# One load for a unit's q and k, row-wise exponentials for its first half, more idle products, and a new order table

## The chip, the cores and the metric

The kernel runs on one core of one Trainium2 chip. Such a core has TensorE for matrix products (PE in the profile; PEld is its loading of weights), VectorE (DVE), ScalarE (ACT), GpSimd (POOL), and SyncE (SP), which here only issues transfers to the 16 DMA engines. The metric is device time in microseconds for one launch. The kernel before was timed three times: 768.71, 768.9 and 770.37 us, median 768.9 us.

## The reference

Chunked attention over q, k and v of 8 batches, 8 heads, 576 positions and 64 dimensions, in chunks of 64, then a two-layer product with a gate:

```python
scores = scale * np.matmul(q_c, k_c.transpose(0, 1, 2, 4, 3))     # per chunk of 64: 64 x 64
scores = scores - np.max(scores, axis=-1, keepdims=True)
attn = np.exp(scores)
attn = attn / (np.sum(attn, axis=-1, keepdims=True) + 1e-09)
out = np.matmul(attn, v_c)
# x: the attention's output as 4608 tokens by 512; w_in 512 x 2048, w_out 2048 x 512
h = x @ w_in
g = h * np.clip(h + 3.0, 0.0, 6.0) / 6.0
return g @ w_out
```

## The kernel before

The 4608 tokens are nine blocks of 512. Each block has two attention units, named by block and half: 00, 01, 10, up to 81. A unit is 128 partitions (two heads of 64) by 8 chunks. Its chain is: load q and k, 64x64 products for the scores, row maximum, exponential, row sum, reciprocal, share (multiply by the reciprocal), turn (transpose), product with v, and keep (copy out of PSUM as x). All the large products are done in float32 as a high and a low part of each operand, with three passes of 128x512: high times high, high times low, low times high (`passes`, L544 to L546). The high part is a ScalarE copy and the low part a VectorE subtraction, so each operand needs one instruction on either engine before its second and third passes can start.

Block 0 is computed directly. Its first products (a0, then eleven more in single passes, L559) begin as soon as unit 00's x and the first weight are there. Blocks 1 to 8 go in four super-blocks (s = 0 to 3) of two blocks, each as a first product of seven quarter-size sums over w_in, gates, and a second product of seven sums over w_out. The operands of the second product are sums of gate tiles: t1 (L1217) and t2 (L1219) are differences and sums of two gate tiles in SBUF, done on GpSimd for s above 0 except where a list gives them to VectorE; m (L1257) are further sums on VectorE; each operand then gets its high copy on ScalarE (L1250, "uh") and its low subtraction on VectorE (L1254, "ul"). The gate itself is L1012, and L1196 adds two PSUM results; both read at least one operand from PSUM.

The order of every engine's instructions is written out: `DATES` holds one number per step, and `Schedule.order` sorts the steps by it. Steps are then issued in that order, each on its own engine, and semaphores hold an engine until the operands of its next instruction are ready. Engines take their instructions strictly in this order, so a step that waits holds all behind it on its engine.

Unit 00 and 01 are special (`class First`): the two heads of a unit are two halves a = 0 and a = 1 of 64 partitions, with own PSUM banks, so that the first half can run ahead. In the kernel before, unit 00's q and k come in two loads of 64 partitions (`load_rows`, L316: step qk00 and step qk00b), and its scores are two steps of 32 products each, one per half. Exponentials of both halves go the same way: a product with minus the identity subtracts the row maximum inside PSUM ("less", L502), one ScalarE instruction takes the exponential of 128x512 (L505), VectorE sums the rows (L508). The other way, by rows, exists for later units and, in `First`, for halves named in `BY_ROWS`, where no half stands yet: VectorE negates the maximum and ScalarE takes eight exponentials of 128x64 with the maximum as bias, each summing its row as it goes.

`warm_up(n)` issues products of a constant with itself that nobody reads: n counts bfloat16 products of 128x512, and four of them are replaced by one float32 product. `WARM` is the count at the program's start. `FILL` scales how many follow a TensorE step, by the planned gap behind it, until block 0's first product with v.

Of the kernel before, what the change touches and what calls it, by code (L numbers as in the profile page):

```python
# [9 lines left out]
F32 = mybir.dt.float32  # L10
# [32 lines left out]
WARM = 8  # L43
APIECE = ['00']
PIECE = 0.75
FILL = (2.0, 4.0)
# [16 lines left out]
LOADS = ['qk00', 'qk00b', 'qk01', 'wa0', 'v00', 'qk10', 'v01', 'wa1', 'wa2', 'wb0', 'v10', 'wa3', 'wb1', 'wa4', 'wb2', 'wb3', 'qk11', 'wa5', 'v11', 'wb4', 'wa6', 'wa7', 'wb5', 'wb6', 'wb7']  # L63
# [16 lines left out]
BY_ROWS = {'00': (), '01': ()}  # L80
# [95 lines left out]
"""  # L176


# [1230 lines left out]
```

## Time and profile before

| | us |
|---|---|
| median of three timed runs | 768.9 |
| the profiled execution, its own time | 769.79 |
| its span, first to last instruction | 768.0 |
| TensorE busy in it | 758.1 (99%) |
| VectorE, ScalarE, GpSimd busy | 586.4, 477.3, 70.6 |

The profile is one execution. Its time lies 0.89 us above the median of the timed runs, and 1.79 us of it lie outside the span. Busy shares are averages: what a stage costs is read from the timelines of that stage. A timeline row gives its start, its length, the engine, the source line, the operation with tile names (buffer numbers left out), shape, and how many equal instructions were merged. In brackets stands the idle time of the engine before it and what ended that. A float32 product shows as two MATMUL instructions, one pass of float32r or bfloat16 as one.

### The profile page before, as it was taken

The numbers are of one execution on the slowest core, as the hardware profiler recorded it, in microseconds if no ns is written. First come the engines' busy times: TensorE is split into PE (matmuls) and PEld (weight loads), VectorE is DVE, ScalarE is ACT, GpSimd is POOL, SyncE is SP. The second block draws the span as 40 slices with busy tenths as digits, with TensorE's granted clock in tenths as the row PEclk, the third lists the DMA queues.
The fourth block names the chain that finished last, engine by engine and source line by source line (L and its number), as shares of the span: only waits on it lengthen the run. The fifth ranks groups of instructions, "written<-read, shape, count | busy, mean of one in ns | idle before, by whom it ended". The sixth has DMA issues, their size and how long they took to land.

```text
span 768.0 us, 13863 instructions
## 1 busy us (share of the span) xinstructions
PE 758.1 (99%) x5443; PEld 621.8 (81%) x5443; DVE 586.4 (76%) x722; ACT 477.3 (62%) x918; POOL 70.6 (9%) x74
## 2 busy tenths in 40 slices
PE   8999999999999999999999999999999999999998
PEld 4788888888888888888888888888888888887787
DVE  3998999988999997636999785456898744368871
ACT  2998878597877756667853646667745444454430
POOL 0000000000000000012100110303000112044001
PEclk9999999999999999999999999999999999999999
DMA  9989999989998786976857586658566665565563
GB/s 316 420 332 351 352 323 339 326 279 294 326 338 306 245 331 204 330 260 207 287 197 258 207 310 224 243 195 276 174 222 217 217 226 191 200 200 182 185 213 117
DMA packets 68321, 200.14 MB, mean 261 GB/s; under 512 B 7136, under 2 KB 19680, under 8 KB 63904
## 3 DMA queue, kind: packets, MB, share of 16 engines
q1 hardware_dynamic: 65632, 191.00, 71.9%
q0 software_dynamic: 2480, 8.13, 2.8%
q8 instruction: 43, 0.70, 0.4%
q14 instruction: 22, 0.18, 0.1%
q10 hardware_dynamic: 144, 0.13, 0.1%
HBM read 154.14 MB, written 45.09 MB: 259 GB/s over the span
## 4 chain that ended last, share of the span: by engine, by line
PE 94%; DVE 4%; DMA 1%; ACT 1%; issue 1%; POOL 0%; DVEq 0%; ACTq 0%
PE acc L544 19%; PE acc L546 18%; PE acc L545 18%; PE h L544 11%; PE h L545 11%; PE h L546 11%; DVE wa L1254 2%; PE two L331 2%; PE h L435 2%; PE h L559 1%; DMA qk<-qk_in 1%; PE s L478 1%; DVE wb L1257 0%; PE two L435 0%; PE s L502 0%
## 5 line engine op out<-in xcount | busy, mean ns | idle before, releaser
L545 PE MATMUL acc<-wa,ws 128*128 128x512 f32 (+1 forms) x432 | 167.5, 388 | 1.2 <-DVE wa L1254 1.2
L544 PE MATMUL acc<-wa,ws 128*128 128x512 f32 (+1 forms) x432 | 168.3, 390 | 0.0
L546 PE MATMUL acc<-wa,ws 128*128 128x512 f32 (+1 forms) x432 | 167.5, 388 | 0.0
L1250 ACT CAST wa<-wb 128x1024 fp32r<-128x1024 f32 x96 | 97.5, 1052 | 59.7 <-DVE wb L1260 19.5
L1254 DVE TENSOR_TENSOR wa<-wb,wa 128x1024 fp32r<-128x1024 f32 x96 | 118.7, 1266 | 19.0 <-ACT wa L1250 19.0
L545 PE MATMUL h<-wa,ws 128*128 128x512 f32 (+1 forms) x248 | 95.8, 386 | 1.0 <-DVE wa L1254 1.0
L1011 ACT ACTIVATE wb<-acc,half 128x512 f32<-128x512 f32 x94 | 64.1, 692 | 52.5 <-DVE acc L1196 48.4
L544 PE MATMUL h<-wa,ws 128*128 128x512 f32 (+1 forms) x248 | 95.7, 386 | 0.0
L546 PE MATMUL h<-wa,ws 128*128 128x512 f32 (+1 forms) x248 | 95.7, 386 | 0.0
L545 PEld LDWEIGHTS acc<-wa,ws 128*128 128x128 f32 x432 | 81.2, 188 | 17.9 <-DVE wa L1254 1.6
L544 PEld LDWEIGHTS acc<-wa,ws 128*128 128x128 f32 x432 | 81.1, 188 | 17.1 <-DVE acc L1196 0.2
L546 PEld LDWEIGHTS acc<-wa,ws 128*128 128x128 f32 x432 | 81.1, 188 | 16.5
L1012 DVE SCALAR_TENSOR_TENSOR wb<-wb,acc 128x512 f32<-128x512 f32 x94 | 62.8, 680 | 24.3 <-ACT wb L1011 24.3
L1196 DVE TENSOR_TENSOR acc<-acc,p 128x512 f32<-128x512 f32 x47 | 32.6, 697 | 55.2 <-PE acc L546 39.6
L545 PEld LDWEIGHTS h<-wa,ws 128*128 128x128 f32 x248 | 46.6, 188 | 10.9 <-DVE wa L1254 1.5
L544 PEld LDWEIGHTS h<-wa,ws 128*128 128x128 f32 x248 | 46.6, 188 | 9.4
L546 PEld LDWEIGHTS h<-wa,ws 128*128 128x128 f32 x248 | 46.6, 188 | 9.3
L366 ACT ACTIVATE e<-two,m 128x64 f32<-128x64 f32 x160 | 48.6, 334 | 7.0 <-DVE m L360 4.9
L1012 DVE SCALAR_TENSOR_TENSOR wb<-wb,h 128x512 f32<-128x512 f32 x34 | 23.1, 683 | 27.6 <-ACT wb L1011 27.5
L1282 POOL DMA_DIRECT2D out_t<-o x17 | 9.4, 553 | 377.5 <-DVE g L1235 235.7
L1217 POOL TENSOR_TENSOR wb<-wb 128x512 f32<-128x512 f32 x18 | 26.0, 1453 | 192.4 <-DVE wb L1012 140.9
L366 ACT ACTIVATION_READ_ACCUMULATOR e<-two,m 128x1 f32 x160 | 36.4, 227 | 0.0
(276 smaller groups left out, 1429.0 us busy)
## 6 DMA issues: line engine op xcount, KB each, us to landing
ws<-b SPq DMA_DIRECT2D x84, 512.0 KB, 4.7
ws<-a SPq DMA_DIRECT2D x72, 512.0 KB, 4.8
qk<-qk_in SPq DMA_DIRECT2D x16, 1024.0 KB, 7.6
wa<-b SPq DMA_DIRECT2D x28, 512.0 KB, 6.9
a<-wa SPq DMA_DIRECT2D x44, 256.0 KB, 5.2
v<-v_in SPq DMA_DIRECT2D x17, 512.0 KB, 6.4
wa<-w_in_out SPq DMA_DIRECT2D x8, 1024.0 KB, 12.3
wb<-w_in_out SPq DMA_DIRECT2D x8, 1024.0 KB, 9.4
```

Of the source, the lines that this page charges most:

```text
L331: PE.matmul(self.s[to, a, 2 * i + k, :], lhsT=self.qk[rows, 0, 2 * i + s, o], rhs=self.qk[rows, 1, 2 * i + s, o], start=True, stop=True)
L366: ACT.activation(out=self.flat(self.e)[:, c], in_=self.flat(self.s)[:, c], func=AF.Exp, bias=self.m[:, c:c + 1], scale=SCALE, accum_out=se ...
L435: PE.matmul(po[s][o, a, i, :], lhsT=self.v[rows, a, i, o], rhs=self.aT[rows, a, i, o], start=not bank or a == i == 0, stop=True, skip_grou ...
L544: PE.matmul(ps, lhsT=a_h, rhs=b_h, start=first, stop=False, skip_group_check=more)
L545: PE.matmul(ps, lhsT=a_h, rhs=b_l, start=False, stop=False, skip_group_check=more)
L546: PE.matmul(ps, lhsT=a_l, rhs=b_h, start=False, stop=last, skip_group_check=more)
L1011: work.add("relu" + name, "ACT", 0.69, [after, *more], lambda: ACT.activation(out=out(), in_=ps(), func=AF.Relu, bias=half, scale=1.0 / 6. ...
L1012: work.add("gate" + name, "DVE", 0.69, ["relu" + name], lambda: DVE.scalar_tensor_tensor(out=out(), in0=out(), scalar=1.0, in1=ps(), op0=A ...
L1196: return lambda: DVE.tensor_tensor(out=t[to], in0=t[of], in1=t["p5"], op=ALU.add)
L1217: work.add(id_("t1."), *on[1:], [id_("gate3."), id_("gate2.")], lambda f=gq, on=on[0]: on.tensor_tensor(out=f(0, 1), in0=f(0, 1), in1=f(0, ...
L1250: ACT.copy(out=g_ops[s, i, pp][:, :, 0], in_=src())
L1254: work.add(low, *(("POOL", 2.5) if on else ("DVE", 1.22)), [high], lambda i=i, pp=pp, src=src, on=POOL if on else DVE: on.tensor_tensor(ou ...
```

## The change

Unit 00's q and k come in one load of 128 partitions; `load_rows`, the two-step scores of unit 00 and the constants for them go. Its first half takes its exponentials by rows. The program starts with 11 units of idle products in place of 8, rounded in another way, and `FILL` is 3.0 in place of 2.0 for gaps up to 3. All of `DATES` is replaced by a new table of 2298 numbers.

```diff
-WARM = 8
-APIECE = ['00']
-PIECE = 0.75
-FILL = (2.0, 4.0)
+WARM = 11
+FILL = (3.0, 4.0)
-LOADS = ['qk00', 'qk00b', 'qk01', 'wa0', ...
+LOADS = ['qk00', 'qk01', 'wa0', ...
-BY_ROWS = {'00': (), '01': ()}
+BY_ROWS = {'00': (0,), '01': ()}
 DATES = """
-0 95 226 357 619 881 1667 ...
+...
-            long = (n + 1) // 4
-            for x in [half] * long + [nought] * max(0, n - 4 * long):
+            long = n // 4
+            for x in [half] * long + [nought] * (n - 4 * long):
-        def load_rows(self, a, qk=None):
-            ...
-        def scores(self, part=(0, 1)):
-            if part[0] == 0:
-                self.s = [t.rearrange("p (c t) -> p c t", t=CH) for t in self.two(ps_b[self.dp])]
+        def scores(self):
+            self.s = [t.rearrange("p (c t) -> p c t", t=CH) for t in self.two(ps_b[self.dp])]
             for c in range(NB):
-                for a in part:
+                for a, rows in enumerate(HALF):
-            if u in APIECE:
-                work.add("scores0" + u, "PE", PIECE, ["qk" + u, *scores], lambda: a.scores((0,)), due=due)
-                work.add("scores" + u, "PE", PIECE, ["scores0" + u, f"qk{u}b"], lambda: a.scores((1,)), due=due)
-            else:
-                work.add("scores" + u, "PE", 1.30, ["qk" + u, *scores], a.scores, due=due)
+            work.add("scores" + u, "PE", 1.30, ["qk" + u, *scores], a.scores, due=due)
```

The first place is TensorE at the program's start, before. `h<-half` are idle products, `s<-qk` the scores of unit 00, `s<-xd` those of unit 01, `s<-m,minus` the subtraction of the maximum.

```order
L247 MATMUL h<-half 128x512 x2
L478 MATMUL s_175<-qk 64x64 x16
L247 LDWEIGHTS half
L247 MATMUL h<-half 128x512
L478 MATMUL s_176<-qk 64x64 x16
L502 MATMUL s_175<-m_162,minus 128x512
L502 MATMUL s_176<-m_163,minus 128x512
L478 MATMUL s_221<-xd 64x64 x2
```

The same place after the change (of the score rows, which alternate between the two halves' banks, the first pair of each unit).

```order
L245 MATMUL h<-half 128x512 x2
L245 LDWEIGHTS half
L245 MATMUL h<-half 128x512
...
L469 MATMUL s_177<-qk 64x64 x2
L469 MATMUL s_178<-qk 64x64 x2
...
L245 LDWEIGHTS half
L245 MATMUL h<-half 128x512
...
L469 MATMUL s_224<-xd 64x64 x2
L469 MATMUL s_225<-xd 64x64 x2
...
L493 MATMUL s_178<-m_166,minus 128x512
L493 MATMUL s_224<-m_169,minus 128x512
L493 MATMUL s_225<-m_170,minus 128x512
```

The first load's scores were two steps with one idle product between; now they are one step, with three idle products behind it, and unit 01's scores stand ahead of every subtraction of a maximum, of which unit 00's first half needs none.

The second place is VectorE at the start, before. `m<-s` is a row maximum, `z<-e` and `z<-xb` are the row sums of unit 00's two halves, the two rows on z that follow add 1e-9 and invert, `e<-e,z` is the share.

```order
L490 TENSOR_REDUCE m_162<-s_175 128x8
L235 TENSOR_SCALAR minus<-ident 128x128
L490 TENSOR_REDUCE m_163<-s_176 128x8
L508 TENSOR_REDUCE z_164<-e 128x8
L511 TENSOR_SCALAR z_164<-z_164 128x8
L512 RECIPROCAL z_164<-z_164 128x8
L515 TENSOR_TENSOR e<-e,z_164 128x512
L490 TENSOR_REDUCE m_166<-s_221 128x8
L490 TENSOR_REDUCE m_167<-s_222 128x8
```

After the change:

```order
L481 TENSOR_REDUCE m_165<-s_177 128x8
L233 TENSOR_SCALAR minus<-ident 128x128
L484 TENSOR_SCALAR m_165<-m_165 128x8
L481 TENSOR_REDUCE m_166<-s_178 128x8
L481 TENSOR_REDUCE m_169<-s_224 128x8
L481 TENSOR_REDUCE m_170<-s_225 128x8
L502 TENSOR_SCALAR z_167<-z_167 128x8
L503 RECIPROCAL z_167<-z_167 128x8
L499 TENSOR_REDUCE z_168<-xb 128x8
L506 TENSOR_TENSOR e<-e,z_167 128x512
```

The sum over `e` is gone, a negation of the maximum is new, and both maxima of unit 01 stand ahead of the first reciprocal.

The third place is the start of the second product of the last super-block (s = 3). First GpSimd, before: its last t1 (L1217, on the last pair of gate tiles) and the t2 (L1219) around it.

```order
L1217 TENSOR_TENSOR wb_1987<-wb_1987 128x512
L1219 TENSOR_TENSOR g_2656<-wb_3875,wb_3848 128x512
L1217 TENSOR_TENSOR wb_1451<-wb_1451 128x512
L1219 TENSOR_TENSOR g_2720<-wb_1658,wb_1451 128x512
L1219 TENSOR_TENSOR g_2656<-wb_3875,wb_3848 128x512
L1219 TENSOR_TENSOR g_2720<-wb_1658,wb_1451 128x512
L1219 TENSOR_TENSOR g_2644<-wb_2090,wb_1987 128x512
```

After the change (t1 is L1202, t2 is L1204):

```order
L1204 TENSOR_TENSOR g_2599<-wb_3874,wb_3860 128x512
L1202 TENSOR_TENSOR wb_1470<-wb_1470 128x512
L1204 TENSOR_TENSOR g_2599<-wb_3874,wb_3860 128x512
L1204 TENSOR_TENSOR g_2704<-wb_1546,wb_1470 128x512
L1202 TENSOR_TENSOR wb_1470<-wb_1470 128x512
L1204 TENSOR_TENSOR g_2681<-wb_2090,wb_2002 128x512
L1204 TENSOR_TENSOR g_2704<-wb_1546,wb_1470 128x512
```

Before, four t2 follow the last t1; now two do, and the other two stand ahead of it. VectorE at the same place, before, from the last gates of the first product on: L1254 is "ul", L1257 is "m".

```order
L1196 TENSOR_TENSOR acc<-acc,p_6755 128x512
L1012 SCALAR_TENSOR_TENSOR wb_1658<-wb_1658,acc 128x512
L1012 SCALAR_TENSOR_TENSOR wb_1451<-wb_1451,acc 128x512
L1254 TENSOR_TENSOR wa_6884<-wb_1987,wa_6884 128x2x512
L1254 TENSOR_TENSOR wa_6860<-g_2681,wa_6860 128x2x512
L1254 TENSOR_TENSOR wa_6872<-wb_1451,wa_6872 128x2x512
L1257 TENSOR_TENSOR wb_1451<-g_2720,wb_1451 128x2x512
L1257 TENSOR_TENSOR wb_3848<-g_2656,wb_3848 128x2x512
L1257 TENSOR_TENSOR wb_3604<-g_2681,wb_3604 128x2x512
L1257 TENSOR_TENSOR wb_1987<-g_2644,wb_1987 128x2x512
L1254 TENSOR_TENSOR wa_6915<-g_2720,wa_6915 128x2x512
L1254 TENSOR_TENSOR wa_6897<-g_2656,wa_6897 128x2x512
```

After the change (L1239 is "ul", L1242 is "m"):

```order
L1239 TENSOR_TENSOR wa_6846<-g_2506,wa_6846 128x2x512
L1181 TENSOR_TENSOR acc<-acc,p_6775 128x512
L997 SCALAR_TENSOR_TENSOR wb_1470<-wb_1470,acc 128x512
L1239 TENSOR_TENSOR wa_6889<-wb_1470,wa_6889 128x2x512
L1239 TENSOR_TENSOR wa_6833<-wb_2002,wa_6833 128x2x512
L1239 TENSOR_TENSOR wa_6901<-g_2599,wa_6901 128x2x512
L1239 TENSOR_TENSOR wa_6933<-g_2681,wa_6933 128x2x512
L1239 TENSOR_TENSOR wa_6924<-g_2704,wa_6924 128x2x512
L1242 TENSOR_TENSOR wb_3618<-g_2506,wb_3618 128x2x512
L1242 TENSOR_TENSOR wb_1470<-g_2704,wb_1470 128x2x512
L997 SCALAR_TENSOR_TENSOR wb_1546<-wb_1546,acc 128x512
L1242 TENSOR_TENSOR wb_3860<-g_2599,wb_3860 128x2x512
```

The four m stood ahead of all but one of the ul that read a t2 (`g`); now four of these stand ahead of every m. For s = 2 GpSimd makes ten such sums in either kernel: before, in the order t1, t1, t1, t2, t1, t1 and four t2, with the sixth on the last pair of gates; now t1, t2, t1, t2, t1, t1, t2, t1, t2, t2, with the second t1 on a pair of gates that VectorE makes late.

## Rows read from the trace of the kernel before

**Rows 1.** The page: busy time by engine, and its group of row-wise exponentials.
```profile
PE 758.1 (99%) x5443; PEld 621.8 (81%) x5443; DVE 586.4 (76%) x722; ACT 477.3 (62%) x918; POOL 70.6 (9%) x74
...
L366 ACT ACTIVATE e<-two,m 128x64 f32<-128x64 f32 x160 | 48.6, 334 | 7.0 <-DVE m L360 4.9
```

**Rows 2.** What TensorE waited for, 24 to 766 us: total, times, longest.
```profile
PE acc L545 <- DVE wa L1254: 1.2, 1, 1.2
PE h L545 <- DVE wa L1254: 1.0, 1, 1.0
```

**Rows 3.** Timeline of TensorE, start: start us, us, line, op, count, [idle before].
```profile
0.93 3.78 PE L247 MATMUL h<-half 128*128 128x512 f32 x4 [0.93 <-DVE half L232]
5.70 1.97 PE L478 MATMUL s<-qk 64*64 64x64 f32 x32 [0.99 <-DMA qk<-qk_in]
...
10.04 3.27 PE L502 MATMUL s<-m,minus 128*128 128x512 f32 x4
13.25 1.16 PE L478 MATMUL s<-xd 64*64 64x64 f32 x64
...
15.30 1.98 PE L502 MATMUL s<-m,minus 128*128 128x512 f32 x4
17.12 0.60 PE L247 MATMUL h<-half 128*128 128x512 bf16 x2
...
24.05 0.47 PE L559 MATMUL h<-xa,wa 128*128 128x512 f32 x1 [0.52 <-DVE wa L283]
```

**Rows 4.** DMA issues of the first 14 us: size, median us to landing.
```profile
qk<-qk_in SPq DMA_DIRECT2D x2, 512.0 KB, 5.8
xd<-qk_in SPq DMA_DIRECT2D x1, 1024.0 KB, 8.5
```

**Rows 5.** Two stretches by engine: us, busy, granted clock, DMA share, GB/s.
```profile
2.00:5.00 3.00, 2.71 (x4) 0.61 (x2) 0.00 (x0) 0.22 (x2) 0.00 (x0) 1.00 1.03 232
7.60:12.00 4.40, 4.40 (x38) 2.81 (x37) 1.52 (x3) 0.00 (x0) 0.00 (x0) 1.00 1.01 417
```

**Rows 6.** Timeline of VectorE, 12 to 24 us.
```profile
12.79 0.69 DVE L508 TENSOR_REDUCE z<-e 128x8 f32<-128x512 f32 x1 [1.93 <-ACT e L505]
...
13.95 0.69 DVE L515 TENSOR_TENSOR e<-e,z 128x512 f32<-128x512 f32 x1
14.56 1.28 DVE L490 TENSOR_REDUCE m<-s 128x8 f32<-128x512 f32 x2
...
17.09 0.69 DVE L508 TENSOR_REDUCE z<-g 128x8 f32<-128x512 f32 x1 [0.22 <-ACT g L505]
```

**Rows 7.** Timeline of ScalarE, 12 to 13 us.
```profile
12.16 0.60 ACT L505 ACTIVATE e<-s 128x512 f32<-128x512 f32 x1 [9.92 <-PE s L502]
```

**Rows 8.** Timeline of TensorE, 703 to 714 us.
```profile
705.94 0.50 PE L545 MATMUL acc<-wa,ws 128*128 128x512 f32 x1 [1.21 <-DVE wa L1254]
...
712.75 0.50 PE L545 MATMUL h<-wa,ws 128*128 128x512 f32 x1 [1.04 <-DVE wa L1254]
```

**Rows 9.** Timeline of GpSimd, 684 to 705 us.
```profile
684.20 1.30 POOL L1217 TENSOR_TENSOR wb<-wb 128x512 f32<-128x512 f32 x1 [8.16 <-DVE wb L1012]
...
697.79 7.00 POOL L1219 TENSOR_TENSOR g<-wb,wb 128x512 f32<-128x512 f32 x4
```

**Rows 10.** Timeline of VectorE, 676 to 716 us.
```profile
684.63 6.41 DVE L1254 TENSOR_TENSOR wa<-wb,wa 128x1024 fp32r<-128x1024 f32 x3
...
703.57 2.31 DVE L1254 TENSOR_TENSOR wa<-wb,wa 128x1024 fp32r<-128x1024 f32 x1
705.81 4.62 DVE L1257 TENSOR_TENSOR wb<-g,wb 128x1024 f32<-128x1024 f32 x4
710.35 3.48 DVE L1254 TENSOR_TENSOR wa<-g,wa 128x1024 fp32r<-128x1024 f32 x3
713.75 2.35 DVE L1254 TENSOR_TENSOR wa<-wb,wa 128x1024 fp32r<-128x1024 f32 x2
```

**Rows 11.** Timeline of GpSimd, 519 to 529 us.
```profile
522.64 5.04 POOL L1219 TENSOR_TENSOR g<-wb,wb 128x512 f32<-128x512 f32 x4
```

More of the change, by code (lines that the diff above doesn't have):

```diff
@@ L62 @@
 KEPT = [f"a{i}" for i in range(8)] + ["b2", "b3", "b6", "b7"]
-LOADS = ['qk00', 'qk00b', 'qk01', 'wa0', 'v00', 'qk10', 'v01', 'wa1', 'wa2', 'wb0', 'v10', 'wa3', 'wb1', 'wa4', 'wb2', 'wb3', 'qk11', 'wa5', 'v11', 'wb4', 'wa6', 'wa7', 'wb5', 'wb6', 'wb7']
+LOADS = ['qk00', 'qk01', 'wa0', 'v00', 'qk10', 'v01', 'wa1', 'wa2', 'wb0', 'v10', 'wa3', 'wb1', 'wa4', 'wb2', 'wb3', 'qk11', 'wa5', 'v11', 'wb4', 'wa6', 'wa7', 'wb5', 'wb6', 'wb7']
 ORDER_W = [name[1:] for name in LOADS if name[0] == "w"]
@@ L310, in load_qk @@
             nc.sync.dma_start(out=self.qk.rearrange("p a c t -> p (a c t)"), in_=qk_in[self.n, self.dp])
-        def load_rows(self, a, qk=None):
-            if not hasattr(self, "qk"):
-                self.qk = qk or ap.tile([P, 2, NB, 2 * CH], F32, name="qk")
-            nc.sync.dma_start(out=self.qk.rearrange("p a c t -> p (a c t)")[HALF[a]], in_=qk_in[self.n, self.dp][HALF[a]])
         def load_v(self, v=None):
@@ L470, in two @@
             return [p.tile([P, NT], F32, name=f"s{a}") for a in range(2)]
-        def scores(self, part=(0, 1)):
-            if part[0] == 0:
-                self.s = [t.rearrange("p (c t) -> p c t", t=CH) for t in self.two(ps_b[self.dp])]
+        def scores(self):
+            self.s = [t.rearrange("p (c t) -> p c t", t=CH) for t in self.two(ps_b[self.dp])]
             for c in range(NB):
-                for a in part:
+                for a, rows in enumerate(HALF):
                     for o in HALF:
-                        PE.matmul(self.s[a][o, c, :], lhsT=self.qk[HALF[a], 0, c, o], rhs=self.qk[HALF[a], 1, c, o], start=c == 0, stop=True, skip_group_check=True)
+                        PE.matmul(self.s[a][o, c, :], lhsT=self.qk[rows, 0, c, o], rhs=self.qk[rows, 1, c, o], start=c == 0, stop=True, skip_group_check=True)
         def places(self):
@@ L876, in attention @@
         if n == 0:
-            if u in APIECE:
-                work.add("scores0" + u, "PE", PIECE, ["qk" + u, *scores], lambda: a.scores((0,)), due=due)
-                work.add("scores" + u, "PE", PIECE, ["scores0" + u, f"qk{u}b"], lambda: a.scores((1,)), due=due)
-            else:
-                work.add("scores" + u, "PE", 1.30, ["qk" + u, *scores], a.scores, due=due)
+            work.add("scores" + u, "PE", 1.30, ["qk" + u, *scores], a.scores, due=due)
             for h in (0, 1):
                 do = lambda name, engine, cost, after, f, h=h: work.add(f"{name}{h}{u}", engine, cost, after, f, due=due)
-                last = do("max", "DVE", 0.69, ["scores" + ("0" if u in APIECE and not h else "") + u, f"max0{u}" if h else None], lambda h=h: a.largest(h))
+                last = do("max", "DVE", 0.69, ["scores" + u, f"max0{u}" if h else None], lambda h=h: a.largest(h))
                 if h in BY_ROWS[u]:
@@ L940, in tile_kernel @@
             work.add(name, "SP", 2.62, (), lambda f=name[1:]: load_w(f), first=k)
-        elif u[:2] in APIECE and part == "qk":
-            work.add(name, "SP", 1.31, [], lambda u=u: heads[u[:2]].load_rows(len(u) - 2, spare.get("qk" + u[:2], lambda: None)()), first=k)
         else:
```

180 rows, old and new, of the table DATES are left out of this document.

## The prediction

> **What bounds the kernel now.** I read the page's busy times first: TensorE works 758.1 of a span of 768.0 us, VectorE 586.4, ScalarE 477.3 [rows 1]. So only what TensorE waits for, or does needlessly, can move the end. The list of its waits from 24 us on is next: it holds two that count, 1.2 and 1.0 us, both for VectorE's L1254, which I call ul [rows 2]. The timeline of TensorE shows the rest of what it loses: the first dense product starts at 24.05 us [rows 3]; behind it, except for those two waits, TensorE runs without a break. So the time is 24.05, plus a dense stretch that the change doesn't alter, plus the stalls, plus 1.79 outside the span (769.79 less 768.0). I sum against the execution of 769.79, and say what the median of 768.9 makes of it.
>
> **How the start comes to 24.05.** Unit 00's first half load frees TensorE at 5.70; its 32 products take 1.97; the second half follows at 8.14; the four subtraction products take 3.27 from 10.04; then unit 01's 64 products take only 1.16 [rows 3]. That is twice as many of the same form in 0.6 of the time: TensorE ran at 1.2 GHz until some point in the subtraction products, and at 2.4 after. (The granted-clock column of the windows shows 1.00 in both stretches [rows 5], so here the durations tell the level, not the column.) Behind the scores the first half's exponential starts at 12.16 [rows 7], and from 12.79 VectorE hardly pauses: its share at 13.95, unit 01's two maxima at 14.56, the sums at 17.09 with 0.22 idle [rows 6], until the first product waits for its L283 at 24.05.
>
> **The change part by part, the start.**
> The load. Two halves of 512 KB landed 5.8 us after their issue, unit 01's whole megabyte at 8.5 [rows 4]; TensorE saw the first half at 5.70. In the early stretch the queues moved 232 GB/s, when only 64-partition transfers were on their way, and 417 when whole ones were [rows 5]. At 417 a megabyte takes 2.5 us, as a half at 232 takes 2.3, so I let the whole load land at 6.0. Bounds: 5.70, as the half, and 8.1, when the second half's products could start. Unit 01's load then lands 2.5 later, at 8.5.
> By the Trainium skill's page "DMA: Bandwidth & Descriptors" (section "Anatomy of one DMA — SWDGE (gpsimd) path") a transfer costs about 2 us and then its bytes at some 436 GB/s; by this the whole load would land 1.2 us behind the half, at 6.9, and the sum would be some 0.8 higher. The trace disagrees in its rates, as the halves ran at little more than half of that figure, so I leave this to the rival on the load.
> Idle products. The four float32 instructions (two products) took 3.78 from 0.93 to 4.71, and 0.99 of waiting followed [rows 3]. Eleven units are two such products and three in bfloat16. One in bfloat16 takes 0.30 when the clock is full (0.60 for two at 17.12 [rows 3]) and about 0.5 before. The warm-up thus ends between 5.6 and 6.3, just as the load lands: TensorE has no pause in its first 6 us. This costs at most 0.3 and takes away the 0.99 in which it did nothing.
> The clock. Before, it was at 1.2 GHz through 3.78 us of full-width products, a pause, and 4.3 us of small score products, and rose within the next full-width ones. Now 5 us of full-width products stand without a break. I take that the clock rises within them (case B); that it rises later, as before, is case A. These are the two ends.
> The chain at 2.4 GHz. Scores of unit 00 6.0 to 7.2 (1.16 [rows 3]); three idle products, 0.9, to 8.1; unit 01's load at 8.5, its scores to 9.7. The first half needs no subtraction, and its eight row-wise exponentials cost 48.6/160, or 0.30, each [rows 1], 2.4 in all, from about 8.1 to 10.5, beside unit 01's load and scores; without that cover they would cost their excess over one 0.60 exponential [rows 7], 1.8. The second half's subtraction takes half of the 1.98 that a full-clock pair took at 15.30 (at the slow clock half of 3.27 [rows 3]): 9.7 to 10.7, exponential to 11.3. From there VectorE's work is known: before, from the maxima's end at 14.56 + 1.2 = 15.76 to 24.05 it took 8.29; the first half's share, 0.61 from 13.95 to 14.56 [rows 6], now stands inside this, and 0.22 of idling goes: 8.7. The first half's sum, increment and reciprocal (1.16, 12.79 to 13.95) and the maxima (1.2) now lie ahead, beside TensorE. First dense product: 11.3 + 8.7 = 20.0, so **4.05 less**.
> The chain at 1.2 GHz. Scores 6.0 to 8.1, idle products to 9.5, scores to 11.6, subtraction 1.63 to 13.0 or 13.2, exponential 13.6, plus 8.7: 22.3, so 1.75 less. What is late next in both is ScalarE's u and r for the first weight, 1.1 to 1.2 each, which stand between the exponentials; I give them nothing, as wa0 (third in the load queue now, fourth before) lands by 11.
>
> **The two stalls.** TensorE idles 1.21 at 705.94 and 1.04 at 712.75 [rows 8], 2.25 in all. The chain of each: GpSimd's t1 and t2 of s = 3 read two operands in SBUF, as ul does; alone such an instruction takes 1.29, beside ul four take 7.00, or 1.75 each [rows 9]. VectorE in its turn: three ul in 6.41 beside GpSimd, 2.31 for the one at 703.57, but 3.48 for three and 2.35 for two when GpSimd is done [rows 10]. So 1.1 is lost per ul that meets GpSimd. Then four m (4.62 from 705.81) stand ahead of the next ul at 710.35 [rows 10], and TensorE waits. The new order puts four ul ahead of the m and two t2 ahead of the last t1. I count both stalls as gone, 2.25 less. Bounds: 0, where the same ul stay late, and 2.57, start to start.
>
> **The rest of the table.** The new table moves most steps by some places. By the order, operands that had room keep some, but for two places that became tighter. At s = 2's second product five GpSimd instructions came in one run (four in 5.04, 1.26 each, hardly disturbed [rows 11]); the new order can make eight of it: between 0 and two stalls like those above, 2.3; I take 0.6, near the undisturbed row. And unit 10's scores moved behind b1, so a second weight is wanted sooner after 24 us: 0 to 0.6, I take 0.2. On SP's queue one load fewer is issued, and all later ones start earlier; a keep step of the weights stands ahead of one load there, with some us of room: nothing, at most a stall of 1 to 2 if the room is gone.
>
> **Sum.** 769.79 − 4.05 − 2.25 + 0.6 + 0.2 = 764.3 (B). Were the start of the median run better than the profiled one by the 0.89 between them, this would be 763.4; I take it that the three times before, from 768.71 to 770.37, already differ by how soon the clock rose, and keep 764.3.
>
> **Rivals.**
> A, the clock rises as late as before: 769.79 − 1.75 − 2.25 + 0.8 = 766.6. For it: 3.78 us of idle products didn't raise it. Against: the next full-width ones did within 3 us, behind work that kept TensorE occupied.
> By the Trainium skill's page "TensorE: Matmul & The Clock Gate" (Part 1) the throttled state is the default "and activity releases the throttle". The trace agrees in that the clock rose once and stayed, but shows that the score products, 4 us of activity by the engine's busy time, did not release it; by the page alone, more idle products speak for B.
> C, the stalls stay or move: the ul that meet GpSimd are slow wherever they stand, and only a stall's place changes. For it: the total of GpSimd's and VectorE's work there is the same. Against: before the stalls four m stood, of which nothing is urgent. 769.79 − 4.05 + 0.8 = 766.5 with the early clock, 768.8 with the late one: 767.7.
> D, slower: the eight GpSimd instructions at s = 2 meet the row of ul there one by one. Each ul then takes 1.1 more, seven take 7.6, and with 1 us of room TensorE loses 6.6: 769.79 − 4.05 − 2.25 + 6.6 + 0.2 = 770.3 with the early clock, 772.6 with the late one. It decides if GpSimd's mean there goes from 1.26 towards 1.75 and over, as in [rows 9]. Against: five went there undisturbed.
> E, the whole load lands late, at 8.1: the halves' slow rate would then be one of the first microseconds and not of 64 partitions. Scores of unit 01 wait until 10.5 as before, and the first dense product comes at 22 to 23.5: 766.3 to 767.8.
>
> **Chances.** B 0.48, A 0.23, C 0.15, E 0.06, D 0.08. A measurement of this kernel tells 0.2%, 1.5 us, from no change: faster is below 767.4, slower above 770.4. B is faster but for 0.02; A for 0.19 of its 0.23; C half; E mostly; D is slower in five of eight. Faster 0.77, same 0.16, slower 0.07. The range from 762.3 (both starts' best, 2.57 for the stalls, no new stall, the median's 0.89 in part) to 768.4 takes in A and most of C; B's own is 762.3 to 766.
>
> **What would show it.** First dense product at 20 (B), 22.3 (A), 22 or later with scores starting at 8 (E); 64 score products in 1.2 against 2.1; row-wise exponentials done before unit 01's scores; no wait for ul above 0.3 around 700 to 715; and no new one where s = 2's second product starts, with GpSimd's instructions there near 1.3. A first product after 23, or more than 2 us of new waits for VectorE anywhere, would make the prediction wrong.

## The result

The changed kernel takes 761.92 us (median of five, 761.74 to 762.11); beside it the kernel before took 769.86 (768.71 to 770.37). The ratio is 0.9901, with a 95% interval of 0.9886 to 0.9915: 7.9 us less. The forecast was 764.3 with a range from 762.3, so the direction held, and most of the mechanism, and the time came out 0.4 us below the range. The profiled execution took 761.94, its span 760.2 us, 7.8 less than before.

TensorE's start in the changed kernel, by the timeline (start, length, line, operation, count, idle time before). Score products are counted here, as in the parts ahead, by MATMUL instructions: 64 of them are 32 products in float32, 16 for each half.

```profile
0.93 4.99 PE L245 MATMUL h<-half 128*128 128x512 f32 x7 [0.93 <-DVE half L230]
5.85 1.16 PE L469 MATMUL s<-qk 64*64 64x64 f32 x64
...
8.24 1.16 PE L469 MATMUL s<-xd 64*64 64x64 f32 x64 [0.47 <-DMA xd<-qk_in]
...
19.35 1.62 PE L550 MATMUL h<-xa,wa 128*128 128x512 f32 x6 [0.39 <-DVE wa L281]
```

The idle products now last until 5.92, and the 64 products of unit 00 take 1.16, as unit 01's do behind them and as unit 01's did in [rows 3] when the clock was up: it is at 2.4 GHz before the first score. The first dense product starts at 19.35, not 24.05. This is **4.70** of the 7.8. The load of 1 MB lands as early as the half did: 5.85 is only when the idle products leave TensorE free, and runs below in which they end sooner start on this load at 5.58 to 5.65. The window that answers to the first of [rows 5] (us, then the busy times, granted clock, DMA share, GB/s) shows the rate:

```profile
2.00:5.00 3.00, 3.00 (x6) 0.97 (x5) 0.00 (x0) 0.23 (x2) 0.00 (x0) 1.00 0.92 350
```

That is 350 GB/s at a DMA share of 0.92, in place of 232 at 1.03. VectorE's chain behind it, by its timeline:

```profile
9.44 1.29 DVE L481 TENSOR_REDUCE m<-s 128x8 f32<-128x512 f32 x2 [0.90 <-PE s L469]
...
11.13 0.69 DVE L499 TENSOR_REDUCE z<-xb 128x8 f32<-128x512 f32 x1
...
16.18 1.22 DVE L275 SCALAR_TENSOR_TENSOR u<-u,r 128x1024 int32<-128x1024 int32 x1
...
18.51 0.69 DVE L281 CAST wa<-u 128x1024 fp32r<-128x1024 f32 x1
```

The pair of maxima stands at 9.44, the second half's sum at 11.13, and from there VectorE has no idle time before the L281 that the first dense product waits for: 8.22 us, where 8.7 was reckoned.

From there on TensorE waits for nothing more. The list that answers to [rows 2], taken from 19 us, has this one entry, the start's own:

```profile
PE h L550 <- DVE wa L281: 0.4, 1, 0.4
```

So the two stalls are gone. What they cost shows in the spacing of TensorE's products before; a product's length overlaps the next one's, so the starts count:

```profile
704.34 0.39 PE L544 MATMUL acc<-wa,ws 128*128 128x512 f32 x1
...
708.60 0.39 PE L544 MATMUL h<-wa,ws 128*128 128x512 f32 x1
...
711.32 0.39 PE L544 MATMUL h<-wa,ws 128*128 128x512 f32 x1
...
713.79 0.39 PE L546 MATMUL h<-wa,ws 128*128 128x512 f32 x1
```

From 708.60 to 711.32 twelve steps take 2.72 undisturbed, 0.227 each. The twelve from 704.34, over the first stall, take 4.26, and the five from 711.32, over the second, 2.47 in place of 1.13. So the stalls cost **2.9**: 2.57 for the two gaps from start to start, and 0.3 because the products behind them also start further apart. At the place where they stood, GpSimd's rows (L1202 is t1, L1204 is t2) and VectorE's (L1239 is ul, L1242 is m) answer to [rows 9, 10]:

```profile
674.82 2.54 POOL L1204 TENSOR_TENSOR g<-wb,wb 128x512 f32<-128x512 f32 x2
...
690.48 3.53 POOL L1204 TENSOR_TENSOR g<-wb,wb 128x512 f32<-128x512 f32 x2
```

```profile
681.35 4.62 DVE L1239 TENSOR_TENSOR wa<-wb,wa 128x1024 fp32r<-128x1024 f32 x4
...
691.64 3.46 DVE L1239 TENSOR_TENSOR wa<-wb,wa 128x1024 fp32r<-128x1024 f32 x2 [2.47 <-ACT wa L1235]
```

GpSimd has done nearly all of its work by 677, in pairs of 2.54, which is 1.27 each; only the last two t2 still meet ul, and take 3.53 where alone they take 2.54. The four ul from 681.35 take 4.62, where three took 6.41; the two from 691.64, beside those t2, take 3.46. About **0.2** of the 7.8 is left; it isn't traced to a cause.

### The profile page after: what moved, and what is told of

It is laid out like the page before. It is cut to its first block, busy times and chain, and to the rows that moved or that the text cites. A ratio compares the mean times of both kernels' runs of the same rounds, so it can differ in the third digit from the quotient of the medians.

```text
span 760.2 us, 13880 instructions
## 1 busy us (share of the span) xinstructions
PE 754.0 (99%) x5448; PEld 619.2 (81%) x5448; DVE 582.4 (77%) x722; ACT 480.2 (63%) x933; POOL 66.2 (9%) x74
## 4 chain that ended last, share of the span: by engine, by line
PE 98%; DVE 1%; ACT 0%; issue 0%; ACTq 0%
PE acc L535 19%; PE acc L537 19%; PE acc L536 19%; PE h L535 12%; PE h L537 12%; PE h L536 12%; PE two L323 2%; PE h L427 2%; PE h L550 1%; PE h L245 1%; PE two L427 0%; ACT e L488 0%; PE acc L427 0%; DVE z L499 0%; DVE xa L448 0%; PE s L469 0%
## 5 line engine op out<-in xcount | busy, mean ns | idle before, releaser
L1239 DVE TENSOR_TENSOR wa<-wb,wa 128x1024 fp32r<-128x1024 f32 x96 | 116.8, 1240 | 20.4 <-ACT wa L1235 20.2
L1202 POOL TENSOR_TENSOR wb<-wb 128x512 f32<-128x512 f32 x18 | 23.0, 1291 | 201.5 <-DVE wb L997 152.6
```

What stands on the lines that cost most here:

```text
L1202: work.add(id_("t1."), *on[1:], [id_("gate3."), id_("gate2.")], lambda f=gq, on=on[0]: on.tensor_tensor(out=f(0, 1), in0=f(0, 1), in1=f(0, ...
L1239: work.add(low, *(("POOL", 2.5) if on else ("DVE", 1.22)), [high], lambda i=i, pp=pp, src=src, on=POOL if on else DVE: on.tensor_tensor(ou ...
```

## The experiments

Each ran beside the kernel before on the same chip; each difference is against the median of before there (769.97 to 770.25). The changed kernel was measured again so, as a yardstick:

> The changed kernel itself, as the yardstick for the two variants of it that run beside it: 761.7 to 762.1 us, first dense product at 19.35.

762.12 us, ratio 0.9899 (0.9885 to 0.9912), first dense product at 19.35.

**The long warm-up, undone in the changed kernel.**

```diff
-WARM = 11
+WARM = 8
-            long = n // 4
-            for x in [half] * long + [nought] * (n - 4 * long):
+            long = (n + 1) // 4
+            for x in [half] * long + [nought] * max(0, n - 4 * long):
```

> The changed kernel with the idle products at the start as before (8 units in the old rounding: two float32 products, no bfloat16 ones). Theory (the unbroken 5 us of idle products let the clock rise before the scores): they end near 4.7, TensorE pauses until 5.85, unit 00's 64 products take about 2.0 us in place of 1.16, and the first dense product comes at about 21.8 us in place of 19.35; time about 764.4 us. Rival (the one load, the row-wise half and the order make the gain at the start; the longer warm-up is incidental): the first dense product stays within 0.4 us of 19.35, time 761.7 to 762.3.

763.22 us, ratio 0.9908 (0.9894 to 0.9922): between the two expectations, 7.0 less than before where the yardstick has 7.9. TensorE's timeline:

```profile
5.60 1.98 PE L469 MATMUL s<-qk 64*64 64x64 f32 x64 [0.89 <-DMA qk<-qk_in]
7.51 1.95 PE L245 MATMUL h<-half 128*128 128x512 f32 x2
9.39 1.16 PE L469 MATMUL s<-xd 64*64 64x64 f32 x64
...
20.49 1.62 PE L550 MATMUL h<-xa,wa 128*128 128x512 f32 x6 [0.38 <-DVE wa L281]
```

The pause is back (0.89), and unit 00's scores take 1.98: so far the theory. But the idle products behind the scores, which in this rounding are one in float32 (1.95), were enough: by unit 01's scores at 9.39 the clock is up, and the first dense product comes at 20.49, 1.14 later than in the yardstick. So the term of the clock holds in kind, and case A was too gloomy, since the idle products between the scores help as well. One of the four runs, at 762.1, is like the yardstick: there the short warm-up may have done, as it did in the next but one experiment; that run has no profile.

**The long warm-up, alone in the kernel before** (the reverse of that edit).

> The kernel before with the 11 units of idle products alone (two float32 and three bfloat16 products). Theory of the clock: the first 32 score products take about 0.6 us in place of 1.97, the subtraction products about half, and the first dense product comes at about 21.5 in place of 24.05, held back now by the second half's load and by unit 01's; time about 767.3. Rival (the start waits for loads anyway): 23.5 to 24.1, time 769.3 to 769.9.

767.96 us, ratio 0.9975 (0.9967 to 0.9984): 2.3 less. The time is near what the theory said, and nine of eleven runs lay between 767.3 and 768.1. The profiled execution, at 770.70, was not one of these, and its first dense product stands at 25.16; the 21.5 of the theory is thus not shown. It shows that the warm-up can be undone. TensorE's timeline, and two of its windows (granted clock third from the end):

```profile
5.79 1.15 PE L478 MATMUL s<-qk 64*64 64x64 f32 x32
...
8.30 1.71 PE L478 MATMUL s<-qk 64*64 64x64 f32 x32 [1.05 <-DMA qk<-qk_in]
9.95 3.78 PE L502 MATMUL s<-m,minus 128*128 128x512 f32 x4
13.65 1.97 PE L478 MATMUL s<-xd 64*64 64x64 f32 x64
```

```profile
9.00:10.00 1.00, 1.00 (x21) 0.88 (x17) 0.00 (x0) 0.00 (x0) 0.00 (x0) 0.50 1.04 434
...
15.00:16.00 1.00, 1.00 (x29) 0.87 (x24) 0.33 (x1) 0.00 (x0) 0.00 (x0) 0.76 1.02 410
```

The first 32 products took 1.15 in place of 1.97, so the clock had risen. Then TensorE waited 1.05 for the second half of the load, and the granted clock fell to 0.50, 1.2 GHz; unit 01's products take 1.97 in place of 1.16, and only in the slice from 15 us does it come back. The pause between two loads may thus be a risk of its own, which the one load removes. This is one execution: waits of 0.75 (the yardstick, ahead of unit 01's scores) and 0.91 us (the row-wise half undone, below) left the clock up, and no run tells the wait apart from the small products around it.

**The one load, alone in the kernel before.**

```diff
-            nc.sync.dma_start(out=...[HALF[a]], in_=qk_in[self.n, self.dp][HALF[a]])
+            if a == 0:
+                nc.sync.dma_start(out=..., in_=qk_in[self.n, self.dp])
```

> The kernel before with unit 00's q and k in one load alone (its second load step issues nothing). Theory (the load pays only when the clock has risen): the first load lands at 5.6 as the half did, the 64 products at 1.2 GHz and the idle one between end near 10.0, as before; first dense product 24.0 to 24.5, time within 0.6 of before. Rival (the load is worth what it brings unit 01's forward, about 2 us, at either clock): first dense product under 23, time 1.2 or more less.

768.86 us, ratio 0.9985 (0.9975 to 0.9996), in two groups: six of twelve runs from 766.8 to 768.1, six from 769.6 to 770.9. The profiled one, 766.77, is of the first:

```profile
0.93 3.78 PE L247 MATMUL h<-half 128*128 128x512 f32 x4 [0.93 <-DVE half L232]
5.58 1.15 PE L479 MATMUL s<-qk 64*64 64x64 f32 x32 [0.88 <-DMA qk<-qk_in]
...
6.98 1.15 PE L479 MATMUL s<-qk 64*64 64x64 f32 x32
```

Here 3.78 of idle products did let the clock rise, in spite of a pause of 0.88 behind them: both halves take 1.15. So with the short warm-up it is a matter of the execution whether the clock rises before the scores: here it did, in the run with the short warm-up above and in the kernel before [rows 3] it did not. The two groups of times fit this, though no run of the slower one has a profile. The theory's "within 0.6" held for five of the six slower runs, the rival's "1.2 or more" for the faster group; what failed in the theory is only that it took the clock to be low. That settles A against B in another way than either was put: the long warm-up makes likely what was chance. It does not make it certain: of eight profiled executions with it, one still has a low clock at the first scores (the three parts together, below).

**Load and long warm-up together in the kernel before.**

> The kernel before with unit 00's q and k in one load (its second load step issues nothing) and the 11 units of idle products; order, exponentials and the waits at 706 and 713 as before. Theory (load and clock make nearly all of the start's gain): scores of both halves end by 7.6, unit 01's by 10.5, first dense product at 20.0 in place of 24.05 to 24.5; time 3.5 to 4.2 less than before. Rival (the row-wise half and the new order make it): first dense product at 21.5 or later, time 2.5 less at most, as with the long warm-up alone.

766.89 us, ratio 0.9961 (0.9949 to 0.9974): 3.1 less, and the five runs lie within 0.8. The first dense product comes at 21.16, neither at 20.0 nor at 21.5:

```profile
5.63 1.15 PE L479 MATMUL s<-qk 64*64 64x64 f32 x32 [0.27 <-DMA qk<-qk_in]
...
8.11 1.99 PE L503 MATMUL s<-m,minus 128*128 128x512 f32 x4
10.03 1.16 PE L479 MATMUL s<-xd 64*64 64x64 f32 x64
...
21.16 1.63 PE L560 MATMUL h<-xa,wa 128*128 128x512 f32 x6 [0.52 <-DVE wa L283]
```

Scores end at 8.1 rather than 7.6, as they are still two steps with an idle product between, and both subtractions stand ahead of unit 01's scores, which start at 10.03.

**The row-wise half, undone in the changed kernel.** Its five steps become three, with the dates shown.

```diff
-BY_ROWS = {'00': (0,), '01': ()}
+BY_ROWS = {'00': (), '01': ()}
+        i = list(self.steps).index("less000")
+        dates[i:i + 5] = [7.20, 7.86, 9.45]
```

> The changed kernel with unit 00's first half by a subtraction product, one exponential and a VectorE sum, as the other halves; the product stands between unit 00's and unit 01's scores. Theory (the row-wise way takes a product of 0.95 off TensorE ahead of unit 01's scores): unit 01's scores start about 0.6 later, first dense product 0.4 to 0.6 later than 19.35, time 762.2 to 762.6. Rival (it is ScalarE's 2.4 us of small exponentials that hold up the second half's): first dense product 0.2 or more earlier, time under 761.7.

763.0 us, ratio 0.991 (0.9896 to 0.9923), 0.9 above the yardstick, but with intervals that overlap; the profiled one, 762.45, is 0.5 above. TensorE's timeline:

```profile
5.65 1.16 PE L471 MATMUL s<-qk 64*64 64x64 f32 x64 [0.20 <-DMA qk<-qk_in]
7.72 1.13 PE L495 MATMUL s<-m,minus 128*128 128x512 f32 x2 [0.91 <-DVE minus L235]
8.78 1.16 PE L471 MATMUL s<-xd 64*64 64x64 f32 x64
...
19.87 1.62 PE L552 MATMUL h<-xa,wa 128*128 128x512 f32 x6 [0.43 <-DVE wa L283]
```

The theory's rows: unit 01's scores at 8.78 in place of 8.24, first dense product 0.52 later. Against the run before it, which also has one load, the long warm-up and no row-wise half, 19.87 stands beside 21.16. These 1.29 are what the rest of the start is worth together: unit 00's scores in one step (they end near 6.8 in place of 8.1), one subtraction ahead of unit 01's scores in place of two, its maxima ahead of the shares, and `FILL`. No run has one of these alone.

**VectorE's order at s = 3, alone in the kernel before.**

```diff
+MOVED = {'ul3.5.3': 695.6, 'ul3.6.3': 698.2, 'ul3.6.1': 698.3, 'ul3.6.2': 698.4}
+        for n, d in MOVED.items():
+            dates[list(self.steps).index(n)] = d
```

> The kernel before with four VectorE steps of s = 3 moved, nothing on GpSimd: the ul of product 5's last pair ahead of that of product 6's first, and three ul that read a t2 ahead of the four m. Theory (VectorE's order decides): both waits of TensorE at 706 and 713 go, though GpSimd still runs beside VectorE there; time 2.3 to 2.6 less than before, about 767.3. Rival (GpSimd's contention decides, the stall moves to the next ul): a wait of 1 us or more stays between 704 and 725, time within 1.2 of before.

768.65 us, ratio 0.9982 (0.9973 to 0.999): 1.6 less. Both old waits are gone and a new one stands at 720, by the list of TensorE's waits and VectorE's timeline (L1257 is ul, L1260 m):

```profile
PE acc L547 <- DVE wb L1015: 1.0, 1, 1.0
```

```profile
700.24 3.69 DVE L1257 TENSOR_TENSOR wa<-wb,wa 128x1024 fp32r<-128x1024 f32 x2 [3.50 <-ACT wa L1253]
...
709.49 4.62 DVE L1260 TENSOR_TENSOR wb<-g,wb 128x1024 f32<-128x1024 f32 x4
...
719.30 0.68 DVE L1015 SCALAR_TENSOR_TENSOR wb<-wb,acc 128x512 f32<-128x512 f32 x1
```

The ul from 700.24 take 1.85 each beside GpSimd; the four m come 3.7 later than in [rows 10], and the gate that TensorE now waits for stands behind all of these, at 719.30. Between the m and the gate stand two ul that wait for ScalarE's copies, and these for the m. VectorE's order passes the loss on, and gives back about half.

**GpSimd's order at s = 3, alone in the kernel before.**

```diff
+MOVED = {'t2.3.3': 670.9, 't1.3.4': 671.0, 't2.3.2': 671.1, 't2.3.4': 671.2, 't2.3.5': 672.0}
```

> The kernel before with five GpSimd steps of s = 3 (one t1, four t2) moved ahead of the t1 that waits for the last but one pair of gates; VectorE's order untouched. Theory of contention: the three ul from 684.6 take 1.2 each in place of 2.1, the one at 703.6 too, and both waits go; about 767.3. Rival (VectorE's order decides, the four m still stand ahead): the second wait of 1.0 us stays, time 768.5 to 769.9.

767.17 us, ratio 0.9962 (0.995 to 0.9974): 3.1 less, and no wait for an ul is left. GpSimd's and VectorE's timelines:

```profile
678.65 3.78 POOL L1222 TENSOR_TENSOR g<-wb,wb 128x512 f32<-128x512 f32 x3
684.35 1.30 POOL L1220 TENSOR_TENSOR wb<-wb 128x512 f32<-128x512 f32 x1 [1.92 <-DVE wb L1015]
```

```profile
684.79 4.21 DVE L1257 TENSOR_TENSOR wa<-wb,wa 128x1024 fp32r<-128x1024 f32 x3
...
701.21 4.62 DVE L1260 TENSOR_TENSOR wb<-g,wb 128x1024 f32<-128x1024 f32 x4
705.76 3.48 DVE L1257 TENSOR_TENSOR wa<-g,wa 128x1024 fp32r<-128x1024 f32 x3
```

The four m still stand ahead of the ul, but start at 701.21, and the ul behind them at 705.76, 4.6 sooner than in [rows 10]. Faster ul make nearly all of this: the three from 684.79 take 4.21 in place of 6.41, and two at 699 and 700 take 1.21 each in place of 2.30 and 2.31. From its first dense product, at 24.41, to the end of its span, 765.3, this execution takes 740.9 us, as the changed kernel does (19.35 to 760.2); the kernel before takes 743.95 (24.05 to 768.0). So GpSimd's order alone brings what the change gains behind the start, and the cause of both stalls was GpSimd's queue: steps that could have run earlier stood behind a t1 that waited 8.16 us for its gate ([rows 9], the bracket at 684.20), and then ran beside the ul.

**Four t2 put back behind the last t1 in the changed kernel.**

```diff
+MOVED = {'t2.3.3': 691.4, 't2.3.2': 691.8}
```

> The changed kernel with two t2 of s = 3 moved behind the last t1, so that four t2 follow it as in the kernel before. Theory (VectorE's new order is not enough where GpSimd meets it, but the work that meets it here is half of before): the ul beside these t2 take 1.7 to 2.3, and TensorE waits less than 0.5: 761.9 to 762.6. Rival (any four t2 behind the last t1 bring a stall back): a wait of 1 us or more between 690 and 720, 763 or more.

761.91 us, ratio 0.9893 (0.988 to 0.9906), no wait. GpSimd's timeline:

```profile
690.36 8.00 POOL L1207 TENSOR_TENSOR g<-wb,wb 128x512 f32<-128x512 f32 x4
```

Its four t2 take 8.00, slower than the 7.00 of before, and it costs nothing. That VectorE has room for it, with the rest of GpSimd's work done early and four ul ahead of the m, is the likely reason; the two weren't told apart here.

**Three parts together in the kernel before:** one load, the long warm-up, GpSimd's order.

> The kernel before with one load, 11 units of idle products and the five GpSimd steps of s = 3 moved ahead, all else as before. If the parts add up: 3.1 less for the first two and 3.1 less for the third (the two sums measured before), so about 763.8 to 764.2, no wait of TensorE for an ul, first dense product at 21.2; what then lacks to the changed kernel, some 1.8, is the row-wise half and the rest of the table. Rival (the parts overlap or the table holds more): over 765.

764.52 us, ratio 0.9924 (0.9911 to 0.9936): 5.45 less where the parts sum to 6.2; between the two expectations. No wait for an ul is left. The 21.2 was missed, by TensorE's timeline:

```profile
0.93 5.06 PE L250 MATMUL h<-half 128*128 128x512 f32 x7 [0.93 <-DVE half L235]
5.92 1.47 PE L482 MATMUL s<-qk 64*64 64x64 f32 x32
...
21.78 1.63 PE L563 MATMUL h<-xa,wa 128*128 128x512 f32 x6 [0.53 <-DVE wa L286]
```

The 32 scores take 1.47, between the 1.15 and the 1.97 of the two levels: here the clock rose only within them, and the start lost 0.6 against the run with the first two parts alone (21.16). About 2.4 remain to the changed kernel. By the first dense products 1.3 of it is the rest of the start, 0.5 the row-wise half and up to 0.6 this late clock, which need not be in the other runs.

**A try to go further:** block 0's four additions of 1e-9 left out.

```diff
-            DVE.tensor_scalar_add(out=self.z[a], in0=self.z[a], scalar1=1e-9)
             DVE.reciprocal(out=self.z[a], in_=self.z[a])
```

> The changed kernel without block 0's four VectorE additions of 1e-9 to the row sums. Each row holds an exponential of about 1, and 1e-9 added to a float32 of 1 or more changes no bit, so the values are the same. Theory (VectorE is the bound from 9.4 to 19.2 us): four instructions of 0.12 to 0.17 and their dependence go, first dense product 0.5 to 0.8 earlier, time 761.1 to 761.4. Rival (ScalarE's or TensorE's chain beside it is as long): 0.2 earlier at most.

762.12 us, ratio 0.9898 (0.9883 to 0.9914): as the yardstick. VectorE's timeline has the reason:

```profile
11.16 0.69 DVE L499 TENSOR_REDUCE z<-xb 128x8 f32<-128x512 f32 x1 [0.28 <-ACT xb L496]
```

The time won at the first addition is lost at 11.16 in a wait of 0.28 for the second half's exponential, which stands on ScalarE behind the eight small ones. In the yardstick this exponential starts at the same time, but there it waits for TensorE's subtraction, as ScalarE's timeline shows:

```profile
10.51 0.60 ACT L496 ACTIVATE xb<-s 128x512 f32<-128x512 f32 x1 [0.24 <-PE s L493]
```

The first dense product comes at 19.06, 0.29 sooner, and the whole gains nothing that can be measured. VectorE is the bound only together with ScalarE and TensorE.

## Why the prediction was off

The likeliest case, B, is the one that came, and both its sources are the ones that were named. That the clock is up at the first score has some luck in it: with the same idle products one execution missed it (1.47, above). The number missed because four terms were mis-sized, all to the same side; with the profiled executions, 764.3 to 761.94:

- The start, 4.05, measured 4.70. The step that failed was "from there VectorE's work is known ... 8.7": it took 8.22. The 8.29 of before held two more waits that went. The additions and reciprocals waited for their operands, 0.2 in all, and other work now stands between. And 0.24 was lost ahead of `u`, with a wait for ScalarE in VectorE's timeline before:

```profile
20.88 1.23 DVE L277 SCALAR_TENSOR_TENSOR u<-u,r 128x1024 int32<-128x1024 int32 x1 [0.16 <-ACT u L270]
```

  After the change `u` starts at 16.18 without one. The rest, 0.17, is unit 01's load, at 8.24 in place of 8.5, with the second half's sum at 11.13 for 11.3. Unit 00's load did not count: in the yardstick its scores start at 5.59 in place of 5.85, and the first dense product stands at 19.35 in both. This load was there at 5.58 in one run, a little below the lower bound of 5.70, and rival E was wrong: the whole megabyte landed no later than the half.
  By the Trainium skill's page "DMA: Bandwidth & Descriptors" (section "Anatomy of one DMA — SWDGE (gpsimd) path") the prediction's estimate had it land at 6.9; that section is on transfers that GpSimd issues, and SP issues this one. The trace disagrees, as TensorE started on it at 5.85.
- The stalls, 2.25, measured 2.9, more than the bound of 2.57. I took the idle time between the lengths of two products; these overlap in an undisturbed run, so from start to start it is 2.57, and the products behind each stall lost another 0.3. The cause was half right. I put VectorE's four m beside GpSimd's contention, and the runs show that without the contention both stalls go though VectorE's order stays (3.1 less), while VectorE's order alone moves the stall (1.6 less). Rival C describes what that run shows.
  By the Trainium skill's page "SBUF — State Buffer" (section "Who interferes with whom") a VectorE instruction with two SBUF inputs contends with a GpSimd one that reads SBUF, and the lock is exclusive; the trace agrees, with 2.31 for an ul beside a t2 [rows 10] and 1.16 each for the four of 4.62 without.
- "Two places became tighter", 0.8, measured 0. GpSimd's run of eight at s = 2 did come about, as its timeline shows:

```profile
514.02 1.29 POOL L1202 TENSOR_TENSOR wb<-wb 128x512 f32<-128x512 f32 x1 [54.50 <-DVE wb L997]
...
519.26 2.15 POOL L1204 TENSOR_TENSOR g<-wb,wb 128x512 f32<-128x512 f32 x1
...
522.74 2.57 POOL L1204 TENSOR_TENSOR g<-wb,wb 128x512 f32<-128x512 f32 x2
```

```profile
518.00 2.27 DVE L1239 TENSOR_TENSOR wa<-wb,wa 128x1024 fp32r<-128x1024 f32 x1 [2.92 <-ACT wa L1235]
```

  But only one t2 of the eight was disturbed (2.15 for one of 1.29), by the one ul that stood beside them on VectorE (2.27), so rival D had no place: no row of ul met them. And TensorE's list shows no wait for a second weight after the start. I had priced a risk as a mean cost, where the likeliest case was nothing.
- The dense stretch, 0, measured some 0.2 less. I called it unaltered.

These make 0.65 + 0.65 + 0.8 + 0.2 = 2.3, the whole miss; the last is what the others leave, so the sum proves nothing of it. The range's low end, 762.3, already took 2.57 and no new stall, but allowed nothing for a start better than 20.0. It stands on 769.79 - 4.05 - 2.57 less the whole 0.89, not a part of it, for a better median; over five runs the kernel before has a median of 769.86, so nothing of that came. What the low end lacked is the start's 0.65 first, and the stalls' 0.3.

The working on the clock was right for this execution but thinner than it looked. I told the level from 32 products in 1.97 against 64 in 1.16, and these are not alike: the 64 alternate between the two halves' rows. At 1.2 GHz the 64 take 1.98 (short warm-up), at 2.4 GHz the 32 take 1.15 (one load), so the clock is a factor of 1.7 and the alternation one of 2. The conclusion stood, since the sum took 64 products at 1.16 and 2.1. One trace of before showed one rise, at some point in the subtraction products; that point varies, as after the same 3.78 us of idle products the first scores ran at the lower level in the short warm-up's profile and at the upper in that of the one load. Changes of this part should be judged by several profiled starts.

## What to carry to other kernels

Where an engine takes its steps strictly in order, look first at what is queued behind a waiting step: GpSimd steps behind one that waited 8 us were the cause of two stalls on another engine. Idle products are to be long enough that the first real ones find the clock up in every run; the eleven units here did so in seven profiled executions of eight. A wait for a second load behind them is better avoided, on the evidence of one execution. When an end stands on two chains of like length, as VectorE's and ScalarE's here, shortening one buys little.

## What was not expected of the hardware

Score products of 64x64 cost by pairs: 64 that alternate between two halves of 64 rows took 1.16, as long as 32 of one half (1.15); so one step in place of two saves the time of one, which the change has from its single load.

With a whole load first, the early stretch moved 350 GB/s against 232 with halves, so 1 MB was there at 5.58 to 5.65 where TensorE waited for it, no later than the 512 KB of 64 partitions at 5.70. And the granted clock, once risen, fell back to 0.50 behind a wait of 1.05 us in one execution, and stayed there for some 7 us, though TensorE was busy in nearly all of them, with the subtraction products from 9.95 on.
